# Four attention steps with token pairs on a partition and products in quarters, and one store moved to ScalarE's queue

## The chip, the core and the metric

The kernel runs on one core of a Trainium2 chip. The metric is device microseconds from start to end of one execution; smaller is better. Engines are named as in the profile: PE is TensorE's matmul side and PEld its weight loads, DVE is VectorE, ACT is ScalarE, POOL is GpSimd and SP is SyncE, which only issues transfers. PEq, SPq and so on are the engines' instruction queues.

## What is computed

Retention (linear attention with a decay for each head) runs over 4 batches, 8 heads, 768 tokens and 64 features. Its output, with the heads side by side, is the input `x` of a mixture of experts: 3072 tokens of 512 features, 8 experts, one expert for each token.

```
state = gamma * state + outer(k[t], v[t])        # for each batch and head, 64 x 64
y[t]  = scale * q[t] @ state
x     = y with heads side by side                # (3072, 512)
e     = argmax(x @ w_gate);  gate = softmax(x @ w_gate)[e]
out   = gate * (relu(x @ w1[e]) @ w2[e])
```

All operands are f32. What is timed here lies almost wholly in the attention stage and in the hand-over to the first expert.

## The kernel before

The decay is split in two: q is multiplied by a rising power of gamma (with the scale) and v by a falling one, both from a table `dec`, so that a step only has to do plain products and a causal mask.

**Steps.** `STEPS` is 12. A step `s` takes 128 tokens of two batches: `where[s] = (m, b1, e)`, where `b1` picks the batches 2*b1 and 2*b1+1, and chunk 2*m+e is a run of 128 tokens. q is loaded for both chunks of an `m` at once, 256 tokens with two neighbours to a partition; k and v are loaded by the chunk, one token to a partition. Steps 0 and 1 are chunks 0 and 1 of the batches 0 and 1; steps 9 and 11 are chunk 5, the last one, of the batches 0, 1 and of the batches 2, 3.

What one step does, for each of its two batches `b`:

- `load` brings q, k and v on SP's queue, some steps ahead. A k or v load is 256 KB, 128 partitions by 8 heads by 64 features, so the runs in DRAM are 64 features long, 256 bytes. A q load has runs of 512 bytes.
- `scale_q` and `scale_v` (lines L521, L527) multiply by the decay, on POOL except for the first.
- `turn_q` and `turn_k` (matmuls at L537, copies by ACT at L550 and L556) bring q and k to features-on-partitions.
- `scores` (L569) makes 64x64 products k.q for each head, on quarters of the array; `mask` (L573, DVE) applies the causal mask and writes `am`.
- `with_state` (L592) adds q times the old state to the output `y`, on quarters of the array.
- `next_state` (L605) makes k.v over 128 tokens, on column halves of the array (128x64); DVE adds it to the state (L609, L611). The last chunk needs none.
- `within` (L623) adds v times `am` to `y`, also on column halves with all 128 tokens; ACT copies `y` to `xT` (L626, L629).
- `to_rows` (L634, DVE) and `store` (L641, SP's queue, four DMAs of 128 KB) write x to DRAM as `x_d`.
- Every second step `logits` (L652, L662) makes the router's logits.

The order on each engine is that of the code (a schedule written by hand); all loads and stores of x share SP's queue, in order. DMAs take eight semaphores in turn, and a DMA waits for the one that had its semaphore before.

**The hand-over.** After steps 5, 9 and 12 (`NEXT`) a `place` generator works out, piece by piece, which expert each token goes to and where; DVE does most of it (L680 to L751) and PE the counts `rk` (L705 to L709) and `found` (L747). With the tokens of steps 0 to 8 placed, step 10 ends with `sources` (`src_e`, L188 to L191), and POOL gathers the first 256 tokens of expert 0 from `x_d` (the early gather, L177, into `xs`). The gather waits for all stores of the steps 0 to 8. Behind it on POOL stand a one-element memset (L756), which holds back the second part of expert 0's first weights until the gather is issued, and the scaling of v for step 11. In step 11 ACT copies the gathered rows to `xe` (L863), PE turns them (`tre`, L807) between the two halves of `within`, and the first layer of expert 0 follows (`hp`, L264). Then come the rest of the routing, the second layer (`yp`, L389) and the other experts.

## Time and profile before

| what | value |
|---|---|
| time of three runs | 450.75 us median (449.15, 450.75, 458.32) |
| the profiled execution | 448.83 us, of which the span of the instructions is 446.9 us |
| busy, share of the span | PE 425.1 us (95%), PEld 84%, POOL 61%, DVE 53%, ACT 28% |
| granted TensorE clock, mean | 0.985 |
| DMA | 80.73 MB, mean 181 GB/s; in the first quarter of the span the DMA engines are busy nine tenths or more in nearly every slice |

The table by stages, the chain of work that ended last and the waits say where an engine stood still; the rows that matter are shown with the prediction. In rows of instructions the columns are the start, the time busy, engine, line, operation, output and input, and in brackets the idle time before it and what ended that.

### The profile page before, as it was taken

What the parts mean: (1) busy time and instruction counts of PE and PEld (TensorE: products, weight loads), DVE (VectorE), ACT (ScalarE), POOL (GpSimd) and SP (SyncE); (2) the same over time, 40 slices, a digit from 0 to 9 for tenths busy, and PEclk for the clock granted to TensorE, in tenths of its full rate; (3) what the DMA queues carried; (4) which work ended last, traced back from release to release, by engine and by line L of the source; (5) the groups of instructions that cost most, each with busy time, mean ns of one, the idle gap of its engine ahead of it and who ended that gap; (6) DMA issues with size and microseconds to landing.
All of it is one profiled execution on the core that took longest, in us unless ns stands there. A gap on an engine that the chain in (4) does not pass through costs nothing.

```text
span 446.9 us, 10588 instructions
## 1 busy us (share of the span) xinstructions
PE 425.1 (95%) x4027; PEld 373.8 (84%) x4027; DVE 237.1 (53%) x541; ACT 124.0 (28%) x285; POOL 271.9 (61%) x226
## 2 busy tenths in 40 slices
PE   7899999997999999999999999799999999999992
PEld 5799888885788779689999998697999999699681
DVE  4454686878389938525652662255356435534320
ACT  2356445362421211313210321024122114112310
POOL 4467525553037479386457958894789698579111
PEclk9999999999899999999999999989999999999997
DMA  9999999988972799368125942774297258120001
GB/s 197 235 238 204 238 243 220 230 195 221 281 230 75 258 396 336 91 240 273 29 69 152 376 128 49 237 289 107 71 301 249 55 167 340 32 91 0 5 29 53
DMA packets 113327, 80.73 MB, mean 181 GB/s; under 512 B 56874, under 2 KB 97834, under 8 KB 113200
## 3 DMA queue, kind: packets, MB, share of 16 engines
q1 hardware_dynamic: 104336, 65.31, 52.5%
q0 software_dynamic: 5520, 12.60, 8.6%
q10 hardware_dynamic: 3344, 1.36, 1.3%
q8 instruction: 52, 0.85, 0.8%
q14 instruction: 75, 0.61, 0.5%
HBM read 60.88 MB, written 15.99 MB: 172 GB/s over the span
## 4 chain that ended last, share of the span: by engine, by line
PE 86%; DMA 4%; DVE 3%; ACT 1%; POOL 1%; SPq 1%; issue 1%; another core or an unknown queue 0%; POOLq 0%; DVEq 0%; ACTq 0%
PE p L343 26%; PE p L389 19%; PE p L277 8%; PE p L264 6%; PE p L983 6%; PE y L623 4%; PE sc L569 4%; PE new L605 2%; PE trk L537 2%; PE yp L389 2%; PE trq L537 2%; PE y L592 2%; DMA w2t<-in_moe_w_dram 2%; DMA q<-in_q_dram 1%; PE parts L652 1%
## 5 line engine op out<-in xcount | busy, mean ns | idle before, releaser
L177 POOL DMA_INDIRECT xs<-x_d,src x30 | 31.9, 1064 | 21.2 <-issue 7.5
L347 DVE TENSOR_TENSOR hT<-p,q 128x196 f32<-128x196 f32 (+5 forms) x72 | 25.5, 359 | 31.2 <-PE p L343 30.5
L573 DVE TENSOR_TENSOR am<-sc,causal 128x512 f32<-128x512 f32 x48 | 29.9, 682 | 20.0 <-PE sc L569 20.0
L343 PE MATMUL p<-t,w1t 128*128 128x196 f32 (+5 forms) x192 | 37.0, 337 | 3.3 <-DVE q L347 3.3
L436 POOL DMA_INDIRECT out_dram<-o,dst x20 | 19.9, 995 | 32.3 <-ACT o L285 12.0
L527 POOL TENSOR_TENSOR vs<-v,dec 128x512 f32<-128x512 f32 x21 | 22.9, 1102 | 24.8 <-DMA v<-in_v_dram 15.5
L277 PE MATMUL p<-w2t,hT 128*24 128x128 f32 (+5 forms) x288 | 37.8, 357 | 0.0
L389 PE MATMUL p<-ws,hs 128*128 128x256 f32 x168 | 37.4, 379 | 0.0
L343 PEld LDWEIGHTS p<-t,w1t 128*128 128x128 f32 x192 | 33.3, 195 | 3.5 <-DVE q L347 3.5
L343 PE MATMUL p<-t,s 128*128 128x196 f32 (+5 forms) x192 | 35.8, 329 | 0.0
L389 PEld LDWEIGHTS p<-ws,hs 128*128 128x128 f32 x168 | 31.9, 190 | 4.3
L395 DVE SCALAR_TENSOR_TENSOR q<-p,gate,q 128x256 f32<-128x256 f32 x28 | 12.8, 480 | 40.3 <-PE p L389 21.1
L521 POOL TENSOR_TENSOR qs<-q,dec 128x512 f32<-128x512 f32 x22 | 22.6, 1054 | 19.0 <-DMA q<-in_q_dram 9.2
L305 POOL TENSOR_TENSOR ws<-w2t,ws 128x1024 f32<-128x1024 f32 x14 | 32.9, 2353 | 0.5
L305 POOL TENSOR_TENSOR ws<-w2t 128x1024 f32<-128x1024 f32 x14 | 33.1, 2364 | 0.1
L347 DVE TENSOR_TENSOR q<-p,q 128x196 f32<-128x196 f32 (+5 forms) x48 | 16.8, 358 | 30.5 <-PE p L343 20.4
L343 PEld LDWEIGHTS p<-t,s 128*128 128x128 f32 x192 | 32.4, 190 | 0.0
L277 PEld LDWEIGHTS p<-w2t,hT 128*24 128x24 f32 (+5 forms) x288 | 18.6, 122 | 16.2 <-issue 15.0
L395 DVE SCALAR_TENSOR_TENSOR o<-p,gate,q 128x256 f32<-128x256 f32 x21 | 10.1, 484 | 34.0 <-PE p L389 25.5
L389 PE MATMUL p<-w2t,hT 128*128 128x256 f32 x112 | 26.9, 381 | 0.1
L569 PE MATMUL sc<-qT,kT 64*64 64x128 f32 x768 | 24.4, 273 | 2.3 <-ACT kT L556 2.3
L983 PE MATMUL p<-hT,w2t 128*128 128x136 f32 (+2 forms) x192 | 25.7, 295 | 0.0
(221 smaller groups left out, 884.6 us busy)
## 6 DMA issues: line engine op xcount, KB each, us to landing
w1t<-in_moe_w_dram SPq DMA_DIRECT2D x7, 2048.0 KB
w2t<-in_moe_w_dram SPq DMA_DIRECT2D x7, 2048.0 KB
k<-in_k_dram SPq DMA_DIRECT2D x24, 256.0 KB
v<-in_v_dram SPq DMA_DIRECT2D x24, 256.0 KB
x_d<-xg SPq DMA_DIRECT2D x48, 128.0 KB
q<-in_q_dram SPq DMA_DIRECT2D x11, 512.0 KB
xs<-xs SPq DMA_DIRECT2D x80, 64.0 KB
w2t<-in_moe_w_dram SPq DMA_DIRECT2D x2, 1024.0 KB
```

The source lines that it names most:

```text
L177: nc.gpsimd.indirect_dma_start(out=xs[:, t, :], out_offset=None, in_=x_d[0:rows, :], in_offset=bass.IndirectOffsetOnAxis(ap=idx[:, t : t + ...
L264: nc.tensor.matmul(hp, lhsT=w1t[:, 0, dt, ts(f, P)], rhs=xT[:, dt, n0:n], start=(dt == 0), stop=(dt == DT - 1))
L277: nc.tensor.matmul(y[j * z : j * z + m, 0:c], lhsT=hT[:, f, t * P + r0 : t * P + r0 + m], rhs=w2t[:, 0, f, ts(j, c)], start=(i == 0), stop ...
L305: by.tensor_tensor(out=ws[i], in0=sums[i][0], in1=sums[i][1], op=ALU.subtract)
L343: nc.tensor.matmul(rows(y), lhsT=a(d, f), rhs=b(d), start=start and d == 0, stop=d == 1, skip_group_check=True)
L347: nc.vector.tensor_tensor(out=to, in0=rows(y), in1=rows(plus), op=ALU.add)
L389: nc.tensor.matmul(y, lhsT=a[:, f, :], rhs=b[:, f, :], start=start and f == 0, stop=f == FH - 1, skip_group_check=True)
L395: nc.vector.scalar_tensor_tensor(out=to, in0=y, scalar=g[i], in1=plus, op0=ALU.mult, op1=ALU.add)
L527: by.tensor_tensor(out=vs, in0=got, op=ALU.mult, in1=inner(dec[:, ts(NC + 2 * where[s][0] + where[s][2], H)], D))
L569: nc.tensor.matmul(sc[j][keys, a, :], lhsT=kT[r, a, keys], rhs=qT[r, a, :], start=True, stop=True)
L573: nc.vector.tensor_tensor(out=am[j], in0=sc[j], in1=middle(causal[:, :], HP), op=ALU.mult)
L983: nc.tensor.matmul(y, lhsT=w2t[:, 0, f, ts(dt, P)], rhs=hT[:, f, EARLY : EARLY + m], start=(i == 0), stop=(i == FT - 1))
```

## The change

- **Layout.** In the steps 0, 1, 9 and 11 (`PAIRED`) the k and v of both batches share one tile: 64 partitions for batch 0 and 64 for batch 1, two neighbouring tokens to a partition, so that the runs in DRAM are 512 bytes. What was "batch b" in these steps becomes "token parity i" for the tiles, and the batch becomes a half of the partitions. All other steps keep their layout, with one tile for both batches.
- **Scaling.** In the four steps POOL scales k (into `ks`) and not v, ahead of the turn; v goes into the products as it was loaded. `dec` has 48 more columns for that. `scale_both(11)` leaves its place behind the early gather and stands at the start of step 10.
- **Products in quarters.** `next_state` (steps 0 and 1) and `within` (all four) have 64 tokens of one batch on a half of the partitions, so that each product is 64x64 on a quarter of the array, in twice as many matmuls; `new` takes two PSUM banks. A second mask `causal2` is made by four more selects on POOL at the start. `within` begins with i = 1 there and ACT copies `y` only at its end.
- **Order.** `y` is kept by batch (bank b) in all steps, so `within` of the other steps does batch 0, copies it, then does batch 1. In the four steps `with_state` stands inside the second `scores`. In step 0 both q are turned first, with DVE scaling both, then both k; `turn_k` of step 1 stands ahead of `within` of step 0.
- **Store.** `store(8)`, the last that the early gather needs, is issued from ACT's queue at the end of step 9, and no longer from SP's queue in the middle of it.

```diff
+PAIRED = (0, 1, 9, 11)
...
+            if s in PAIRED:
+                nc.sync.dma_start(raw[nm, s][ts(b, P // 2), :].rearrange("p (h r) -> p h r", h=H),
+                                  got.rearrange("h (t e) d -> t h (e d)", e=2))
...
+        def scale_kv(s, i, by=nc.gpsimd):
+            c = 2 * where[s][0] + where[s][2]
+            got, nm, c = ("k", "ks", 2 * NC + 2 * CP.index(c) + i) if s in PAIRED else ("v", "vs", NC + c)
+            if i == 0:
+                raw[nm, s] = att.tile([P, 2 * H * D], F32, tag="vs", name=nm)
+            by.tensor_tensor(out=half_of(nm, s, i), in0=half_of(got, s, i), op=ALU.mult, in1=inner(dec[:, ts(c, H)], D))
...
+            if s in PAIRED:
+                new = [ps(*tag, "new")[:, 0 : HP * D].rearrange("p (a d) -> p a d", a=HP) for _ in range(2)]
+                for i in range(2):
+                    kt, vs = keys(s, i), values(s, i)
+                    for a in range(HP):
+                        for b, j in ((0, 0), (1, 1), (0, 1), (1, 0)):
+                            h, rows = 2 * a + j, ts(b, P // 2)
+                            nc.tensor.matmul(new[b][ts(j, D), a, :], lhsT=kt[rows, h, :], rhs=vs[rows, h, :],
+                                             start=(i == 0 and a == 0), stop=(i == 1), skip_group_check=True)
...
+                    if s in PAIRED:
+                        for b, j in ((0, 0), (1, 0), (0, 1), (1, 1)):
+                            rows = ts(b, P // 2)
+                            nc.tensor.matmul(place_of(y, b, a, j), lhsT=vs[rows, 2 * a + j, :], rhs=am[i][0][j][rows, a, :],
...
-                scale_both(STEPS - 1)
...
+            if s + 1 in PAIRED:
+                scale_both(s + 1)
...
-                if s == NEXT[NR - 1]:
-                    store(s - 1)
...
+            if s == NEXT[NR - 1]:
+                store(s - 1, nc.scalar)
```

How the rows stand on the engines, at three places. In them `trq` and `trk` are the turns of q and k, `sc` the scores, `new` the next state, `y` the output, `lg` and `parts` the logits, `tre` the turn of the gathered rows, `hp` the first layer.

PE, step 0, from its first turn to its first product for `y`; before:

```order
L537 MATMUL trq<-ident,qs 128x128 x8
L537 MATMUL trk<-ident,k 128x128 x4
L569 MATMUL sc<-qT,kT 64x128 x16
L537 MATMUL trq<-ident,qs 128x128 x8
L537 MATMUL trk<-ident,k 128x128 x4
L569 MATMUL sc<-qT,kT 64x128 x16
L605 MATMUL new<-vs,k 64x64 x16
L623 MATMUL y<-am_196,vs 64x128
```

and now, up to the turns of step 1's k and the first product:

```order
L568 MATMUL trq<-ident,qs 128x128 x16
L568 MATMUL trk<-ident,ks 128x128 x8
L602 MATMUL sc<-qT,kT 64x128 x32
L648 MATMUL new<-v,ks 64x64 x32
L568 MATMUL trk<-ident,ks 128x128 x8
L680 MATMUL y<-am_243,v 64x128 x2
```

Both batches' q stand ahead of any k, `new` has 32 matmuls where it had 16, and the turns of step 1's k have come ahead of `y`.

PE, step 11, from the scores to the turn of the gathered rows (the matmuls of `y` that only repeat are left out); before:

```order
L569 MATMUL sc<-qT,kT 64x128 x32
L763 LDWEIGHTS ones_b
L763 MATMUL tot<-acc,ones_b 128x2
L652 MATMUL parts<-xT,wg 32x256 x8
L592 MATMUL y<-qT,state_1981 64x128 x16
L662 MATMUL lg<-ident,lgT 128x128 x4
L623 MATMUL y<-am_2036,v 64x128
```

and now:

```order
L602 MATMUL sc<-qT,kT 64x128 x28
L624 MATMUL y<-qT,state_2023 64x128 x16
L602 MATMUL sc<-qT,kT 64x128 x4
L823 LDWEIGHTS ones_b
L823 MATMUL tot<-acc,ones_b 128x2
L713 MATMUL parts<-xT,wg 32x256 x8
L723 MATMUL lg<-ident,lgT 128x128 x4
L680 MATMUL y<-am_2115,v 64x128 x2
```

The product with the state has moved from between `parts` and `lg` into the scores, and `y` takes v as it was loaded.

POOL, from the last piece of the routing in step 9 to the early gather; before:

```order
L696 CAST told<-less 128x8
L527 TENSOR_TENSOR vs<-v,dec 128x512 x2
L177 DMA xs_112<-x_d,src_e 128x512 x2
L756 MEMSET w1t 1x1
L527 TENSOR_TENSOR v<-v,dec 128x512 x2
```

and now:

```order
L757 CAST told<-less 128x8
L554 TENSOR_TENSOR ks<-k,dec 128x512 x2
L554 TENSOR_TENSOR vs<-v,dec 128x512 x2
L192 DMA xs_74<-x_d,src_e 128x512 x2
L817 MEMSET w1t 1x1
```

Step 11 is scaled ahead of step 10, and nothing is left behind the gather. On ACT the four stores now stand between the copies of step 9's `y` and the turns of step 11's k.

More of the change, by code (lines that the diff above doesn't have):

```diff
@@ L37, in decay_table @@
     back = [gamma ** -(P * c + i + 1) for c in range(NC)]
+    two = 2 * (i % (P // 2))
+    back += [gamma ** -(P * c + two + e + 1) for c in CP for e in range(2)]
     return np.concatenate(on + back, 1).astype(np.float32)
@@ L96 @@
     x_d = dram.tile([N, Q * DT * L], F32, tag="x_d", name="x_d")
-    dec = const.tile([P, 2 * NC * H], F32, tag="dec", name="dec")
+    dec = const.tile([P, 2 * (NC + len(CP)) * H], F32, tag="dec", name="dec")
     wg = const.tile([P, DT, P // DT], F32, tag="wg", name="wg")
     ident = const.tile([P, P], F32, tag="ident", name="ident")
-    ones = const.tile([P, P], F32, tag="ones", name="ones")
+    causal2 = const.tile([P, 2, P], F32, tag="causal2", name="causal2")
+    first = ctx.enter_context(tc.tile_pool(name="first", bufs=1))
+    xs2 = [first.tile([P, TC, Q * DT * L], F32, tag=f"xs{i}", name=f"xs{i}") for i in range(2)]
+    ones = xs2[0][:, 0, 0:P]
     causal = const.tile([P, P], F32, tag="causal", name="causal")
@@ L114 @@
                             pattern=[[1, P]], channel_multiplier=-1)
+    for b in range(2):
+        for e in range(2):
+            rows = ts(b, P // 2)
+            nc.gpsimd.affine_select(out=causal2[rows, e, :], in_=ones[rows, :], compare_op=ALU.is_ge, fill=0.0, base=-e,
+                                    pattern=[[1, P]], channel_multiplier=-2)
     nc.gpsimd.memset(ones_b, 1.0)
@@ L170, in weights @@
         return weights1(pool, e), weights2(pool, e)
-    first = ctx.enter_context(tc.tile_pool(name="first", bufs=1))
-    xs2 = [first.tile([P, TC, Q * DT * L], F32, tag=f"xs{i}", name=f"xs{i}") for i in range(2)]
     def gather(xs, idx, tiles, rows=N):
@@ L496 @@
             warm(P)
-        where = [(s // 4, s // 2 % 2, s % 2) for s in range(STEPS)]
+        where = [place_of_step(s) for s in range(STEPS)]
         raw, front, state, x = {}, {}, {}, {}
@@ L605, in next_state @@
                         nc.tensor.matmul(new[ts(j, D), b, a, :], lhsT=kt[:, h, :], rhs=vs[:, h, :], start=True, stop=True)
-            old = state.get(b1)
-            state[b1] = att.tile([P, 2, HP, D], F32, tag=f"state{b1}", name=f"state{b1}")
-            if old is None:
-                nc.vector.tensor_copy(state[b1], new)
-            else:
-                nc.vector.tensor_tensor(out=state[b1], in0=new, in1=old, op=ALU.add)
+            add(now, new, old)
         def within(s, y, am, between=lambda: None):
@@ L635, in to_rows, with store @@
                                     x[s][:, :, b, :].rearrange("p a (r l) -> p a r l", l=L))
-        def store(s):
+        def store(s, queue=nc.sync):
             m, b1, e = where[s]
@@ L825 @@
                     scale_q(s + 2, b)
-            if s + 2 < STEPS and s != NEXT[NR - 1]:
+            if s + 1 < STEPS and s + 1 not in PAIRED and s != NEXT[NR - 1]:
                 scale_both(s + 1)
@@ L831, with old_state @@
                 nc.gpsimd.memset(xs2[s % 2], 0.0)
+            y = outputs()
+            def old_state():
+                if where[s][0] or where[s][2]:
+                    with_state(s, y)
             if s:
-                am = [scores(s, b) for b in range(2)]
+                am = [scores(s, 0), scores(s, 1, old_state if s in PAIRED else lambda: None)]
                 am[0][1]()
@@ L843 @@
                 logit = logits(steps)
-            if where[s][0] or where[s][2]:
-                with_state(s, y)
+            if s not in PAIRED:
+                old_state()
             def ahead():
@@ L890 @@
             step(s, "b")
+            if s == 0:
+                ahead()
             within(s, y, am, early_rows if s + 1 == STEPS else lambda: step(s, "w"))
@@ L952 @@
         pair(hTa, wa[1], S, T, oa, egates, lambda: fetch_ahead(which, 0),
-             lambda name: att.tile([P, FH * P], F32, tag="v", name=name, bufs=8)[:, 0:DH], some,
+             dict(zip(("m10", "m11", "u20", "u21", "u3"), (pe[:, ts(i, DH)] for pe in [
+                 att.tile([P, 2 * FH * P], F32, tag="v", name="pe", bufs=4) for _ in range(3)] for i in range(2)))).get, some,
              (("sc", 4), ("sc", 4), ("y", 2), ("y", 2), ("tr", 2), ("tr", 2)))
```

144 lines of the change are left out of this document (83 added, 61 removed).

## The prediction

> **What bounds the kernel now.** I read the table by stages first, then the chain that ended last, then the rows at the places where that chain leaves PE. The stages are cut where PE begins step 1's scores (18.17), where DVE takes up the routing of steps 5 to 8 (91.08), where PE begins step 11 (104.32), at the first `hp` (117.01) and at the third product of `yp` (136.51).
>
> ```profile
> 0.00:18.17 18.17, 14.09 (x166) 10.56 (x166) 6.90 (x16) 6.62 (x11) 7.60 (x24) 1.00 1.08 220
> 18.17:91.08 72.91, 72.07 (x1593) 64.23 (x1594) 47.01 (x93) 35.53 (x65) 40.60 (x43) 1.00 1.01 227
> 91.08:104.32 13.24, 11.61 (x233) 10.21 (x231) 12.14 (x38) 6.00 (x12) 5.54 (x9) 1.00 0.88 200
> 104.32:117.01 12.69, 9.72 (x160) 7.25 (x158) 7.61 (x25) 4.06 (x7) 4.34 (x5) 0.87 0.88 246
> 117.01:136.51 19.50, 19.30 (x105) 15.74 (x104) 14.05 (x45) 5.58 (x14) 6.34 (x9) 1.00 0.78 224
> 136.51:446.90 310.39, 298.28 (x1776) 265.79 (x1776) 149.34 (x326) 66.16 (x178) 207.46 (x139) 0.98 0.49 161
> ```
>
> A row gives the stretch, its length, the busy time of PE, PEld, DVE, ACT and POOL, the granted clock, the DMA share and GB/s. Steps 1 to 8 are PE's own time: 72.07 of 72.91 us are busy. The DMA engines are full there too (1.01), so a transfer that gets shorter gives nothing at once; it lands earlier. Behind 117.01 the change edits little (two temporaries share a tile), and PE is busy 19.30 of 19.50 us, so what is won or lost ahead of `hp` should reach the end unchanged. Room is at the head (4.1 us without PE), in step 10 (1.6 us) and in step 11 (3.0 us, at a clock of 0.87). For step 11 the chain says why:
>
> ```profile
> 104.45 3.58 DMA v<-in_v_dram
> 108.03 1.24 POOL xs L177
> ...
> 110.67 2.02 POOL v L527 x2
> 112.73 1.02 PE y L623 x8
> 113.75 1.91 PE tre L807 x8
> 115.66 1.35 PE y L623 x16
> 117.01 1.92 PE hp L264 x8
> ```
>
> The early gather starts at 108.03, v of step 11 is scaled behind it, and PE's products wait for that. The rows of the timeline around it show what the gather itself stood waiting for:
>
> ```profile
> 94.53 1.31 DVE L634 STREAM_TRANSPOSE xg<-xT 128x512 f32<-128x512 f32 x2
> 95.43 8.35 SPq L641 DMA_DIRECT2D x_d<-xg  x12
> 104.36 0.17 DVE L191 TENSOR_SCALAR src_e<-tok_e 128x2 uint32<-128x2 f32 x1
> 112.60 0.62 ACT L863 COPY xe<-xs 128x512 f32<-128x512 f32 x1 [4.37 <-DMA xs<-x_d,src_e]
> 113.87 0.62 ACT L863 COPY xe<-xs 128x512 f32<-128x512 f32 x1 [0.65 <-DMA xs<-x_d,src_e]
> ```
>
> The rows to gather were known at 104.53. Step 8's x was ready at 95.84, but its store is the last four of the twelve that SP worked off until 103.78, in line behind older ones; so the 3.5 us to 108.03 are the landing of these stores (the chain puts them down to a v load issued next, which shares semaphores with them).
>
> **The change, part by part.**
>
> *Transfers.* The first row below is a stretch with 256-byte packets alone, the second one (14.4 to 16.4 us) with 512-byte packets nearly alone.
>
> ```profile
> DMA packets 3720, 0.82 MB, mean 205 GB/s; under 512 B 3720, under 2 KB 3720, under 8 KB 3720
> DMA packets 1144, 0.59 MB, mean 297 GB/s; under 512 B 16, under 2 KB 1143, under 8 KB 1143
> ```
>
> k and v of a paired step are 1 MB: 5.1 us at 205 GB/s, 3.5 us at 297. Two such steps stand at the head of the queue (3.2 us) and two near its end (3.2 us). Everything that SP issues behind step 1 comes about 3 us earlier, and the v of step 10, for which POOL and then PE waited, 4 to 5 us.
>
> *Head.* These rows of the chain and of the timeline carry the old and the new one:
>
> ```profile
> 2.40 5.78 DMA q<-in_q_dram
> 4.37 1.59 DVE L521 TENSOR_TENSOR qs<-q,dec 128x256 f32<-128x256 f32 x4 [2.90 <-DMA q<-in_q_dram]
> 7.06 0.64 ACT L550 COPY qT<-trq 128x512 f32<-128x512 f32 x1 [4.47 <-PE trq L537]
> 7.80 0.59 ACT L556 COPY kT<-trk 128x512 f32<-128x512 f32 x1
> 12.16 1.04 POOL L527 TENSOR_TENSOR vs<-v,dec 128x512 f32<-128x512 f32 x1 [1.79 <-DMA v<-in_v_dram]
> 12.26 1.10 PE sc L569 x32
> 13.36 1.08 PE new L605 x32
> ```
>
> Before, the second q landed at 8.18, as the 1280th KB. Now both halves of k stand ahead of it: 1536 KB at the higher rate, some 0.7 us later, about 8.9. DVE then scales its last half (0.8 us), PE turns it, ACT copies (0.64): 10.5. POOL's four more selects end at 4.5, k has landed by 7.2, `ks` is done at 9.3, off the path. The turns of k and the copy to `kT` (0.59) bring the first scores to 11.4 and their end to 13.3, where they ended at 13.36 before. `new` (priced below at 1.91) ends at 15.2. k of step 1 lands near 13 and is scaled by 15.1, so that its turns run 15.2 to 16.2, `y` until 18.1, and step 1 starts then: **0.0 us** against 18.17. Bounds: 0.7 earlier if `new` costs what it did; 2 us later if k of step 1 lands 2 us later than I have it, since POOL's scaling and the turns are in its line.
>
> *Products in quarters.* Step 3 has all kinds of product in a row:
>
> ```profile
> 33.40 1.91 PE sc L569 x64
> 35.31 0.87 PE y L592 x32
> 36.18 1.00 PE parts L652 x16
> 38.20 0.44 PE lg L662 x4
> 40.39 1.08 PE new L605 x32
> 41.47 1.75 PE y L623 x32
> ```
>
> The trace counts two passes to a matmul. A quarter pass costs 29.8 ns in the scores and 27.2 ns in `y L592`. `y L623` has 32 passes on column halves, 54.7 ns each; in quarters 64 passes at 29.8 ns are 1.91 us, 0.16 more. `new` has 32 passes of half the length at 33.8 ns each; in quarters 64. No row shows quarter passes of 64 columns. If four of them run side by side as the long ones do, the cost stays 1.08 us; if a pass takes no less time than any quarter pass of the trace does, it is 1.91. I take 1.91, since 1.08 would need 16.9 ns a pass, half of the shortest seen in these rows. The Trainium skill ("TensorE: Matmul & The Clock Gate", Back-to-back issue gap) gives a floor of about 25 ns from start to start however short a matmul is: by it `new` would be estimated at 1.6 us and the sum 0.3 us lower; no row here decides between them. Step 1 is on PE's dense stretch: +0.83 and +0.16, **+1.0 us**. Step 9's +0.16 falls into PE's idle time of step 10, where DVE is last.
>
> *DVE's chain.* From 91.08 to 104.53 DVE sets the pace (12.14 of 13.24 us busy, ending with `src_e`). It starts 1.0 later. One piece of it was slow before, while POOL scaled v of step 9 beside it; the second row is the same operation later, alone:
>
> ```profile
> 91.66 0.72 DVE L681 TENSOR_TENSOR dl<-lg,mx 128x64 f32<-128x64 f32 x1
> 121.32 0.21 DVE L681 TENSOR_TENSOR dl<-lg,mx 128x48 f32<-128x48 f32 x1
> ```
>
> POOL scales k of step 9 already in step 8 now: **-0.5 us** (bounds 0 and 0.5). `src_e` ends at 105.0.
>
> *Store and gather.* ACT issues store(8) behind the copies of step 9's `y`, about 97 to 99.5, and it lands some 2 to 3 us later, ahead of 105.0. Behind it on ACT wait the copies of step 11's `kT`, needed by PE at 104.8: hidden, with 4 us to spare. SP's last half of store(7), v of step 11 and the first weights wait for semaphores that these four DMAs hold, until about 102; the weights are needed at `hp`, so that is hidden as well. The gather starts at 105.1 and not at 108.03: **-2.9 us** with the two terms above in it.
>
> *From the gather to `hp`.* Before, 8.98 us. The two halves of the gathered rows landed 4.57 and 5.84 us behind its start, so now `xe` is there at 110.3 and 111.6. PE starts step 11 at 104.8; scores with the state 2.8, `parts` 1.2 with the small count, the copy of the logits, now bare, 0.6, `lg` 0.44, half of `y` 0.95: 110.9, so nothing waits for v any more. The turns take 0.5 each at full clock, the second from 111.6; the other half of `y` ends at 113.1, where `hp` starts: 8.0 us, **-1.0 us**. It rests on the clock, too:
>
> ```profile
> 113.00:114.00 1.00, 1.00 (x10) 0.67 (x7) 0.00 (x0) 0.35 (x2) 0.00 (x0) 0.50 1.10 368
> ```
>
> After PE's pause the clock was half and the turns took 1.91 us; with PE at work until 110.9 I take it as full. If it is not, 1 us is lost.
>
> **Sum.** `hp` at 113.1 against 117.01: -3.9 us, so 448.83 - 3.9 = 444.9 for the profiled execution (span 443.0). That execution is the lowest of those shown; the other two near it, 449.15 and 450.75, are on average 1.1 above it. I predict 446.
>
> **Rivals.**
>
> 1. *Quarter passes of 64 columns run side by side.* `new` stays at 1.08, step 1 starts 0.7 earlier and costs 0.16 more. DVE's chain is 1.0 earlier than before instead of 0.5 later, so 443.4 in the sum, 444.5 as a time. For it: quarters do overlap in two rows. Against: 16.9 ns a pass is seen nowhere. 17%.
> 2. *The store gains nothing by its new queue.* store(8) moves at the pace of what SP has queued, or ACT is held by a semaphore whose last DMA is still in SP's line; then the gather starts near 108.0 as before and `hp` 8.0 later, at 116.0: 447.8, or 449 as a time. For it: the DMA share is 0.88 in that stretch and ACT's four DMAs wait for DMAs of SP's. Against: 3 us less of line by then. The Trainium skill ("DMA: Bandwidth & Descriptors", Issuing engines are not separate DMA queues) says that all queues share the same 16 engines and a second issuer saves only issue time, which is this rival; the row of twelve stores shows that time to be 8.35 us. 18%.
> 3. *Slower: quarters with all tokens of two batches do not overlap.* Passes cost 54.7 ns in `y` and 33.8 in `new`. Step 0 gives +1.75, step 1 +2.83, step 9 +1.3 in DVE's chain, step 11 +0.8: `hp` at 118.8, 1.8 late, 450.6, or 451.7 as a time. It loses from some 47 ns a pass on, on a line between 29.8 (-3.9) and 54.7 (+1.8). Against: two kinds of quarter product run below 30 ns. 10%.
>
> My forecast has 55%.
>
> **Range.** The forecast with its bounds (head -0.7 to +2, clock +1) is 445 to 449; to hold eight in ten it reaches over rivals 1 and 2 and their spread: 442 to 450.5. 2% is 9 us (about what a measurement of this kernel can tell from no change), and no case comes near it: within 92%, faster 5%, slower 3%.
>
> **What would show it.** Step 1's scores start near 18.1; its `new` takes 1.9 us and `y` 1.9; `src_e` ends near 105, the gather starts with it and no longer waits for a DMA; no half clock around step 11; `hp` near 113. I am wrong if PE waits for `trk` of step 1 or 9, if the gather still waits for stores, or if the stages behind `hp` change in length.

## The result

The changed kernel takes 452.25 us (median of 20 runs), the kernel before 449.87 us (20 runs on the same chip): a ratio of 1.0132 with a 95% interval of 1.0098 to 1.0165. I had said 446, 442 to 450.5; the change made the kernel slower by some 1%, where I expected 1% faster. In some executions the granted clock is lower and the time some per cent longer; the ratios leave these out, and the profiles of b_store and best6 below are such executions, so that their ratios count and their stages are only a hint.

The profiled execution after took 452.17 us (span 450.5), the one before 448.83 (446.9). These two differ by 3.6 us of span, the medians by 2.4; the ratio stands for some 5.9 us. What follows explains the 3.6; the two profiles don't say where the rest of the 5.9 lies. The table by stages, cut at the same events as before:

```profile
0.00:21.66 21.66, 15.91 (x231) 12.01 (x235) 9.78 (x21) 4.76 (x7) 12.05 (x31) 0.84 1.03 245
21.66:95.61 73.95, 71.75 (x1666) 64.18 (x1659) 50.35 (x95) 36.87 (x67) 36.98 (x39) 1.00 0.95 231
95.61:110.11 14.50, 12.22 (x265) 10.50 (x263) 13.02 (x37) 6.00 (x12) 5.23 (x9) 1.00 0.60 147
110.11:120.14 10.03, 8.61 (x192) 6.40 (x190) 7.45 (x22) 3.37 (x6) 2.33 (x3) 1.00 0.68 222
120.14:139.90 19.76, 19.76 (x108) 16.36 (x108) 14.78 (x50) 6.15 (x15) 6.56 (x10) 1.00 0.76 205
139.90:450.50 310.60, 297.67 (x1775) 263.57 (x1773) 148.69 (x326) 65.84 (x178) 207.01 (x138) 0.99 0.48 161
```

| stage | before | after | difference |
|---|---|---|---|
| head, until PE begins step 1 | 18.17 | 21.66 | +3.49 |
| steps 1 to 9, until the routing chain on DVE | 72.91 | 73.95 | +1.04 |
| routing chain, until step 11 | 13.24 | 14.50 | +1.26 |
| step 11, until `hp` | 12.69 | 10.03 | -2.66 |
| `hp` to the third `yp` | 19.50 | 19.76 | +0.26 |
| rest | 310.39 | 310.60 | +0.21 |

In the table above, the row "steps 1 to 9" hides two opposite terms: step 1 takes 1.34 us and step 8 1.29 us longer, while steps 4 and 6 take 6.63 and 6.64 us instead of 7.06 and 8.12.

**The head.** The chain that ended last (first fence), the timeline (second) and three stretches of the table by windows (third; the third number from the end is the granted clock):

```profile
8.54 2.16 DVE qs L546 x2
...
10.75 1.54 PE trq L568 x6
12.29 1.71 PE trk L568 x8
13.99 1.83 PE sc L602 x32
```

```profile
8.19 2.22 POOL L554 TENSOR_TENSOR ks<-k,dec 128x512 f32<-128x512 f32 x2 [3.63 <-DMA k<-in_k_dram]
8.54 2.82 DVE L546 TENSOR_TENSOR qs<-q,dec 128x256 f32<-128x256 f32 x4 [1.17 <-DMA q<-in_q_dram]
9.56 0.69 PE L568 MATMUL trq<-ident,qs 128*128 128x128 f32 x2 [3.12 <-DVE qs L546]
```

```profile
8.00:9.00 1.00, 0.00 (x0) 0.00 (x0) 0.46 (x1) 0.00 (x0) 0.81 (x1) 0.84 1.20 286
9.00:14.50 5.50, 4.44 (x28) 3.67 (x32) 3.05 (x5) 1.68 (x3) 1.75 (x3) 0.50 1.23 245
15.00:16.00 1.00, 1.00 (x36) 1.00 (x32) 0.15 (x1) 0.00 (x0) 1.00 (x2) 0.75 1.15 341
```

The second q landed at 8.5, forecast was about 8.9. But DVE needs 2.82 us for its four products, 1.59 before: POOL scales k over the first two. PE has nothing to do for 3.12 us, and its clock is half from 8.7 to 15.5 us, so that eight turns of k take 1.71 us and half the scores 1.83, where 1.0 to 1.1 each is usual.

**Step 1.** From the chain:

```profile
28.59 1.09 PE new L648 x64
29.68 1.31 PE y L680 x48
30.99 0.92 issue
31.91 0.67 PE y L680 x16
```

`new` in quarters takes no longer than in halves (1.09 us, 17 ns a pass). Inside `y` PE stands still for 0.92 us and waits for nothing that the trace shows (such a row is called "issue"); before, no such gap stood in step 1. Some 0.4 us more goes ahead of the products with the state: a weight load waits 0.39 us for ACT's copies of step 0's `y`, all three of which now come at its end.

**Steps 8 to 10.** The timeline:

```profile
80.85 5.08 DVE L792 TENSOR_SCALAR here<-rrow,prow 128x128 bf16<-128x128 bf16 x10
81.79 2.09 POOL L554 TENSOR_TENSOR ks<-k,dec 128x512 f32<-128x512 f32 x2 [4.14 <-issue]
83.84 4.04 POOL L546 TENSOR_TENSOR qs<-q,dec 128x512 f32<-128x512 f32 x4
86.58 0.85 PE L808 MATMUL found<-val,here 128*128 128x160 bf16 x10 [1.13 <-DVE am L608]
...
98.42 0.22 DVE L751 TENSOR_REDUCE gate<-ex 128x8 f32<-128x64 f32 x1 [1.00 <-ACT ex L743]
100.41 2.05 POOL L554 TENSOR_TENSOR ks<-k,dec 128x512 f32<-128x512 f32 x2
100.93 0.54 DVE L778 TENSOR_TENSOR acc<-acc,seen 128x8 bf16<-128x8 bf16 x1
101.47 1.02 DVE L783 TENSOR_SCALAR prow<-ranks 128x8 int32<-128x8 int32 x1
102.41 2.25 POOL L554 TENSOR_TENSOR vs<-v,dec 128x512 f32<-128x512 f32 x2
102.61 1.15 DVE L785 TENSOR_TENSOR at<-ohs,is_col 128x256 f32<-128x256 bf16 x1
```

Before, the same ten `here` and the same `gate` stood like this; `acc`, `prow` and `at` took 0.17, 0.17 and 0.43:

```profile
77.66 3.35 DVE L731 TENSOR_SCALAR here<-rrow,prow 128x128 bf16<-128x128 bf16 x10
93.89 0.22 DVE L690 TENSOR_REDUCE gate<-ex 128x8 f32<-128x64 f32 x1 [0.51 <-ACT ex L682]
```

Each long row of the kernel after stands beside a scaling on POOL. The first rows cost PE 1.13 us in step 8, the others lie in the chain to `src_e`.

**Step 11.** The gather follows the rows to gather at once (timeline); behind it PE's chain has three short gaps (chain):

```profile
110.31 0.17 DVE L206 TENSOR_SCALAR src_e<-tok_e 128x2 uint32<-128x2 f32 x1
110.78 1.24 POOL L192 DMA_INDIRECT xs<-x_d,src_e  x1 [6.12 <-DMA w1t<-in_moe_w_dram]
```

```profile
111.87 0.23 issue
...
112.69 0.19 issue
...
113.35 0.30 issue
```

### The profile page after: what moved, and what is told of

Its sections match the earlier page's. It is cut to its first block, busy times and chain, and to the rows that moved or that the text cites. A ratio compares the mean times of both kernels' runs of the same rounds, so it can differ in the third digit from the quotient of the medians.

```text
span 450.5 us, 10959 instructions
## 1 busy us (share of the span) xinstructions
PE 425.9 (95%) x4219; PEld 373.0 (83%) x4219; DVE 244.1 (54%) x547; ACT 123.0 (27%) x284; POOL 270.2 (60%) x229
## 3 DMA queue, kind: packets, MB, share of 16 engines
q10 hardware_dynamic: 4432, 1.91, 1.7%
## 4 chain that ended last, share of the span: by engine, by line
PE 88%; DVE 5%; DMA 2%; issue 2%; ACT 1%; SPq 1%; POOLq 0%; DVEq 0%
PE p L358 25%; PE p L404 19%; PE p L292 8%; PE p L279 6%; PE p L1049 6%; PE sc L602 4%; PE hp L279 3%; PE yp L404 3%; PE y L684 3%; PE trk L568 2%; PE trq L568 2%; PE y L624 2%; PE new L659 1%; PE y L680 1%; PE parts L713 1%
## 5 line engine op out<-in xcount | busy, mean ns | idle before, releaser
L410 DVE SCALAR_TENSOR_TENSOR q<-p,gate,q 128x256 f32<-128x256 f32 x28 | 12.8, 480 | 42.5 <-PE p L404 29.5
L410 DVE SCALAR_TENSOR_TENSOR o<-p,gate,q 128x256 f32<-128x256 f32 x21 | 10.2, 484 | 33.8 <-PE p L404 28.5
L669 ACT COPY xT<-y 64x512 f32<-64x512 f32 (+1 forms) x36 | 20.9, 581 | 24.3 <-PE y L684 17.9
L554 POOL TENSOR_TENSOR vs<-v,dec 128x512 f32<-128x512 f32 x16 | 16.6, 1055 | 17.1 <-DMA v<-in_v_dram 17.0
L1049 PEld LDWEIGHTS p<-hT,w2t 128*128 128x128 f32 x192 | 25.5, 190 | 0.0
```

The lines of the kernel that those rows point to most:

```text
L410: nc.vector.scalar_tensor_tensor(out=to, in0=y, scalar=g[i], in1=plus, op0=ALU.mult, op1=ALU.add)
L669: nc.scalar.copy(out=x[s][rows, :, b, :], in_=y[b][other, :, :])
L1049: nc.tensor.matmul(y, lhsT=w2t[:, 0, f, ts(dt, P)], rhs=hT[:, f, EARLY : EARLY + m], start=(i == 0), stop=(i == FT - 1))
```

## The experiments

Four questions: the head, PE's gap in step 1, POOL beside DVE in steps 8 to 11, and the store. The chips differ between groups, so ratios go against runs of the kernel before on the same chip, and stages are read from each run's profile. One profile stands for each run, and small differences between two of them are no effect of an edit: best2 and best2_sp differ in nothing ahead of step 9, yet the routing chain begins 2.03 us apart (90.92 and 92.95), and a gap of 1.77 us in step 4 of best2_sp makes most of it. Ratios of different chips can't be compared finely either: after, h_dvek and s_sp bring `hp` within 1 us of each other and have 1.0132, 1.0065 and 1.0076.

| run | step 1 begins | step 1 takes | chain begins (`lg`) | `lg` to end of `src_e` | `src_e` to `hp` | `hp` | ratio (95%) |
|---|---|---|---|---|---|---|---|
| before | 18.17 | 9.40 | 91.08 | 13.45 | 12.41 | 116.94 | 1 |
| after | 21.66 | 10.74 | 95.61 | 14.87 | 9.59 | 120.07 | 1.0132 (1.0098-1.0165) |
| h_warm | 19.67 | 11.35 | 94.22 | 14.86 | 9.23 | 118.31 | 1.0131 (1.0048-1.0214) |
| h_dvek | 20.99 | 11.58 | 96.03 | 14.85 | 9.59 | 120.47 | 1.0065 (1.0031-1.0099) |
| h_both | 19.20 | 12.17 | 97.62 | 14.88 | 9.59 | 122.09 | 1.0094 (1.0055-1.0133) |
| p_oldhead | 18.55 | 9.17 | 93.20 | 14.87 | 9.59 | 117.66 | 1.0035 (1.0001-1.0069) |
| p_01 | 22.58 | 12.40 | 98.57 | 14.21 | 9.68 | 122.46 | 1.0085 (1.0042-1.0127) |
| e_fill | 21.40 | 9.24 | 94.01 | 14.88 | 8.82 | 117.71 | 1.0083 (1.0041-1.0125) |
| r_noks | 20.36 | 10.74 | 92.63 | 14.12 | 8.56 | 115.31 | 0.9973 (0.9930-1.0015) |
| r_early | 20.94 | 11.57 | 96.25 | 12.96 | 9.62 | 118.83 | 1.0037 (0.9998-1.0076) |
| best1 | 18.05 | 9.30 | 93.94 | 13.93 | 9.60 | 117.47 | 1.0025 (0.9981-1.0069) |
| best2 | 18.42 | 9.17 | 90.92 | 16.30 | 9.80 | 117.02 | 1.0023 (0.9969-1.0077) |
| best2_sp | 18.54 | 9.56 | 92.95 | 17.39 | 9.77 | 120.11 | 0.9995 (0.9954-1.0037) |
| best6 | 23.79 | 10.20 | 95.61 | 14.13 | 8.15 | 117.89 | 1.0078 (1.0042-1.0113) |
| best4 | 18.00 | 9.20 | 92.32 | 14.49 | 9.58 | 116.39 | 1.0039 (1.0003-1.0076) |
| best5 | 18.09 | 9.39 | 94.34 | 14.14 | 8.16 | 116.64 | 0.9979 (0.9933-1.0025) |
| s_sp | 20.36 | 11.30 | 95.07 | 14.86 | 9.60 | 119.53 | 1.0076 (1.0029-1.0122) |
| b_store | 18.66 | 9.98 | 92.62 | 15.15 | 8.81 | 116.58 | 1.0013 (0.9965-1.0061) |

### The head: h_warm, h_dvek, h_both, p_oldhead

h_warm, in the changed kernel:

```diff
             scale_q(0, b, nc.vector, 2)
+            for _ in range(3 * b):
+                warm(512)
             turn_q(0, b, 2, (nc.scalar.copy, nc.vector.tensor_copy))
```

> Three more idle products on PE between the two turns of q, so that PE doesn't pause while DVE scales the second q. Theory A (after PE's pause the granted clock is half from 9 to 14.7 us, and that stretches the turns of k from 1.02 to 1.91 us, the last turns of q and the scores): the clock stays 1.0, step 0's scores end near 14.5 instead of 16.6, and step 1's scores start near 20.0 instead of 21.55; DVE's scaling of the second q stays at 2.82 us. Rival B (the longer order alone costs the 3.4 us: both q and both k must be scaled and turned before any score): the clock is full but step 1 starts within 0.5 us of 21.55.

h_dvek:

```diff
-        scale_both(0)
...
         scale_q(0, 1, nc.vector, 2)
+        for i in range(2):
+            scale_kv(0, i, nc.vector)
         turn_q(0, 1, 2, (nc.scalar.copy, nc.vector.tensor_copy))
```

> Step 0's k is scaled by DVE behind its second q, so that POOL does nothing while DVE scales. Theory (POOL's scaling of k from 8.19 to 10.41 holds up DVE's four products of the second q, 2.82 us for them instead of 1.57): they take 1.6 us again, the turns of q end about 1.2 us earlier, and step 1's scores start near 20.5, though k is now scaled by 11.7 instead of 10.4. Rival (DVE is slow there for another cause, such as a q that lands in pieces): the four still take 2.8 us, k is ready at 12.9, and step 1 starts at 23 or later.

h_both has both edits.

> Both mends of the head in one kernel: three idle products on PE while it waits for the second q, and step 0's k scaled by DVE behind that q instead of by POOL beside it. If the clock and the lock-out are the two costs of the head and they add: the clock stays at 1.0, DVE needs 1.6 us for the second q, and step 1 starts near 18.7 to 19.3 (old head: 18.1 to 18.6; the three idle products alone: 19.67). Rival (the longer order costs the rest, and k by DVE comes later than k by POOL): step 1 starts at 19.7 or later, no earlier than with the idle products alone.

p_oldhead: `PAIRED = (9, 11)`, with the loads, order and scalings of the head as before the change.

> Only steps 9 and 11 have two tokens to a partition; steps 0 and 1 stand as in the kernel before, with its loads and its order at the head; the store of step 8 stays on ACT's queue. If the head and step 1 are where the time went (3.38 and 1.5 us by the two traces): step 1's scores start near 18.2 as before, the routing chain starts near 91.5, hp near 116, and the time is 4 to 5 us under the changed kernel's, 1 under the kernel's before or level with it. Rival (the longer stages of steps 8 to 10 follow from the later transfers of steps 0 and 1 or from their PE time, and the gain in step 11 rests on the shorter transfers of steps 0 and 1): step 1 starts at 18.2, but hp at 117.5 or later.

The same stretch of windows in h_warm, and DVE's first two products for the second q in h_both:

```profile
9.00:14.50 5.50, 5.04 (x81) 3.58 (x81) 3.41 (x7) 1.72 (x3) 1.85 (x2) 1.00 1.23 266
```

```profile
8.44 0.76 DVE L546 TENSOR_TENSOR qs<-q,dec 128x256 f32<-128x256 f32 x2 [1.05 <-DMA q<-in_q_dram]
```

With PE kept at work the clock stays at 1.00 and step 1 begins at 19.67; the six runs with this head and no mend of the clock began it between 20.36 and 22.58 (p_01's 22.58 has a gap of 1.14 us in it; best6's head is another one). So the half clock costs 0.7 to 2 us, by when it falls and how long it lasts: 6.83 us from 8.67 on in the changed kernel, 3.41 us from 10.60 and 10.71 on in s_sp and r_noks, whose heads are the same program and begin step 1 at 20.36. The 2 us are the dear end of it. With nothing on POOL beside them two products take 0.76 us, where the changed kernel's first two took 2.16. In h_dvek itself this bought little: the second half of q landed only at 10.5, PE paused as long, and the clock was half from 11.26 to 14.68; h_both, with both mends, begins at 19.20, 0.5 ahead of h_warm. The old head stands at 18.0 to 18.7 in seven runs. So of 3.5 us the clock is the largest part, POOL's holding up of DVE about half a microsecond once the clock is mended, and 0.5 to 1.2 us the longer order (both q before any score).

p_oldhead, where step 1 begins at 18.55 and takes 9.17 us, is rid of three quarters of the loss up to `hp` (0.72 us of 3.13 are left; its ratio is 1.0035). Still `hp` comes at 117.66 and not at 116, as its rival had said: its chain takes 14.87 us as in the changed kernel. The two mends of the longer head don't show in the time: h_both's `hp` is the second latest of the table. Its lead is lost in steps 1 and 8. In step 8, which takes 11.12 us there and 8.62 in the changed kernel, `here` takes 6.04 us beside POOL, PE waits 2.08 us, and the clock is half from 87.21 to 90.62. What went wrong behind the head is the next question.

### PE's gap in step 1: p_01, e_fill, and the other runs

p_01: `PAIRED = (0, 1)`; steps 9 to 11 and the store as in the kernel before.

> Only steps 0 and 1 have two tokens to a partition; steps 9 to 11, their scalings and the store on SP's queue stand as in the kernel before. If the head, step 1 and POOL's scaling of k of step 9 are the losses: step 1 starts at 20.4 to 21.7, step 8 takes 7.3 us again, the chain of routing 13.3, and the transfers of the first steps, some 3 us ahead, let v of step 11 land early; hp near 118.5 to 119.5, the time 1.5 to 2.5 us over the kernel's before. Rival (the lead of the transfers is the gain, and steps 9 and 11 only cost): hp at 117 or earlier and the time level with or under the kernel's before.

e_fill, in p_oldhead, at the start of steps 0 and 1:

```diff
+            if s < 2:
+                quarters(32)   # 32 products 64x64x16 on idle data, one bank for each row half
             y = outputs()
```

> Steps 9 and 11 paired, steps 0 and 1 as in the kernel before, and ahead of each of these two 32 idle products of 64 x 64 x 16 on PE, which write nothing that is used: as many instructions as the quarters of steps 0 and 1 add. Theory (PE runs out of fetched instructions): a gap of 0.9 to 2.5 us with nothing to wait for appears in step 1, some 16 passes ahead of the end of its y, which is in halves here, and ends about 1 us behind the landing of the packet of the instruction queue; step 1 takes 10.5 to 12 us from scores to scores instead of 9.2. Rival (the gap belongs to the quarters): no gap, step 1 takes 9.2 to 9.5 us beside the idle products, which stand ahead of its scores and cost 1 to 2 us there.

In all runs with steps 0 and 1 paired (here h_warm, h_both, p_01, s_sp) the gap is there, and always at the same place of PE's program:

```profile
28.21 1.49 PE L680 MATMUL y<-am,v 64*64 64x128 f32 x48
31.17 0.67 PE L680 MATMUL y<-am,v 64*64 64x128 f32 x16 [1.47 <-issue]
```

```profile
30.42 1.49 PE L680 MATMUL y<-am,v 64*64 64x128 f32 x48
34.49 0.67 PE L680 MATMUL y<-am,v 64*64 64x128 f32 x16 [2.57 <-issue]
```

```profile
27.61 1.47 PE L680 MATMUL y<-am,v 64*64 64x128 f32 x42
30.51 0.77 PE L680 MATMUL y<-am,v 64*64 64x128 f32 x19 [1.43 <-issue]
```

The first is s_sp, the second p_01: 48 passes of `y`, then the gap, then 16. The third is h_warm, which has three more products (six passes) ahead of it: the gap comes after 42 passes, and the last three of 64 have a row of their own. After h_both's three it is 42 too. A wait on data would not move by six passes. The queues of the DMA engines show what does come in steps of the program, here in the changed kernel from 29.5 to 31.0:

```profile
q8 instruction: 1, 0.02, 3.9%
```

One packet of 16 KB, busy for 0.9 us (3.9% of 16 engines in 1.5 us), on a queue that the profile calls "instruction". Narrower windows put its start at 29.7. Found in the same way in ten profiles (before, where the gap is the 0.72 us in step 6; after; h_warm, h_dvek, h_both, p_01, r_noks, r_early, s_sp, best6), such a packet landed 1.3 to 1.55 us ahead of the end of the gap, while the gaps' ends lie between 30.5 and 34.5 us in the paired ones. It holds for more than step 1: between 10 and 125 us of the 18 profiles PE has 24 gaps of over 0.32 us that wait for nothing, in 15 of the profiles, and each ends 1.28 to 1.59 us behind the landing of a 16-KB packet of this queue. Some shorter ones, as the three in step 11, have no such packet just ahead. I take it that PE has run out of fetched instructions there; the packets and the place of the gap speak for it, though it is inferred and no run took a packet away.

The expectation for e_fill failed in part: step 1 took 9.24 us without a gap. In step 0 it has one:

```profile
15.20 1.91 PE L691 MATMUL y<-am,vs 128*64 128x128 f32 x31
17.86 0.32 PE L691 MATMUL y<-am,vs 128*64 128x128 f32 x1 [0.74 <-issue]
28.79 1.92 PE L691 MATMUL y<-am,vs 128*64 128x128 f32 x32
```

It stands near the end of step 0's `y`, where the changed kernel (0.33 us, 9 passes ahead of the end) and p_01 (1.14) have their first one. So the number of instructions alone brings the first gap, and not the second; why the second packet comes late in the paired steps stays open. What it costs is in the table: step 1 takes 9.2 to 10.0 us unpaired and 10.2 to 12.4 paired. A quicker head may only wait longer (h_both 2.25 us, ending at 30.86; the changed kernel 0.92, ending at 31.91), though r_noks, 1.3 us ahead, waits 0.92 as well.

p_01 says the same of the whole: the two paired steps at the head alone bring `hp` to 122.46. That is 3 us later than expected, with four gaps of this kind (1.14, 2.57, 0.45 and 0.79 us) and a half clock from 111.45 to 114.86. Its rival, that the lead of the transfers is a gain, fell for the whole; a part of it may be real, since in the nine kernels with steps 0 and 1 paired step 6 takes 6.6 us, and 6.6 to 8.4 in the others.

### POOL beside DVE: r_noks, r_early, best1, best2, best6, best4, best5

r_noks, in the changed kernel, leaves out the factor on k in steps 9 and 11 (`keys` gives the raw k there, its tokens in another order), so that its output is not that of the program:

```diff
-            if s + 1 in PAIRED:
+            if s + 1 in PAIRED and s < 8:
                 scale_both(s + 1)
```

> Leaves out the scaling of k in steps 9 and 11 on POOL (the products take the raw k, and its tokens in another order): PE and DVE have the same work, POOL 4 us less. Theory (POOL's scaling holds up DVE's operations beside it): the ten rows of here in step 8 take 3.3 us instead of 5.08 and PE no longer waits 1.1 us for am behind them; of the routing chain acc 0.54, prow 1.02 and at 1.15 go back to 0.17, 0.17 and 0.43, unless the scaling of v of step 10 moves beside them; the chain starts near 94.3 and the rows to gather are known 2 to 3 us earlier than 110.48. Rival (DVE is slower there for its own order, or PE is what it waits for): here stays at 5 us and the chain ends within 0.5 us of 110.48.

r_early:

```diff
-                raw[nm, s] = att.tile([P, 2 * H * D], F32, tag="vs", name=nm)
+                raw[nm, s] = raw["v", s] if s in (8, 10) else att.tile([P, 2 * H * D], F32, tag="vs", name=nm)
...
+            if s == NEXT[NR - 1]:
+                scale_both(STEPS - 1)
+                scale_both(s + 1)
```

> The changed kernel with POOL's scalings of late moved clear of DVE's small operations: v of steps 8 and 10 is scaled in place, so that k of step 9 needs no buffer that is still read and is scaled near 78 to 80, ahead of here, and k of step 11 and v of step 10 in step 9, ahead of the routing chain or beside its first operations, not beside acc, prow and at. The head is unchanged. Lock-out theory: here x10 takes 1.9 to 3.4 us instead of 5.08, acc, prow and at 0.17, 0.17 and 0.43, val starts 1.5 us earlier behind own, and from step 1's start to hp it takes 3.5 to 5 us less than the changed kernel's 98.4. Rival (PE and ACT hold the chain, DVE's slow rows only fill its slack): the rows get short and hp moves by less than 1.5 us.

The rows of r_noks, then those of r_early:

```profile
79.22 1.90 DVE L794 TENSOR_SCALAR here<-rrow,prow 128x128 bf16<-128x128 bf16 x10
97.40 2.05 POOL L554 TENSOR_TENSOR vs<-v,dec 128x512 f32<-128x512 f32 x2
98.46 1.01 DVE L785 TENSOR_SCALAR prow<-ranks 128x8 int32<-128x8 int32 x1
```

```profile
101.56 0.17 DVE L778 TENSOR_TENSOR acc<-acc,seen 128x8 bf16<-128x8 bf16 x1
101.72 0.17 DVE L783 TENSOR_SCALAR prow<-ranks 128x8 int32<-128x8 int32 x1
```

Without k's scaling beside them the ten `here` take 1.90 us instead of 5.08, and `at`, now alone, 0.42; `prow`, beside v's scaling, still takes 1.01. Step 8 takes 7.33 us again, as before, and not 8.62. The time falls: against h_dvek on the same chip, which differs in the head, the ratio is lower by 0.0092, some 4 us, and `hp` comes 5.2 us earlier; how much of the time comes from the other output, with other routing behind it, wasn't separated. The rows of `here` themselves need no such care. Over all 18 profiles the ten take 1.70 to 1.90 us where POOL scales nothing or next to nothing beside them, 2.74 to 3.35 beside two scalings, 4.23 to 5.20 beside three or four, and 6.04 in h_both. In r_early no scaling stands beside `acc`, `prow` and `at`, all are short (`at` 0.42), and the chain takes 12.96 us, 1.9 less than in the changed kernel and 0.5 less than before. In step 8 r_early gained nothing: k of step 9 is scaled from 78.2, but the q of step 10 then follows on POOL beside `here`, which takes 5.20. By its own measure the expectation failed: from step 1 to `hp` it takes 97.89 us, 0.5 less than the changed kernel's 98.41 and not 3.5 to 5, and `hp` moved by 1.24 us, which the rival allowed. But steps 1 and 8 are 0.83 and 0.48 us longer there; from `lg` to `hp`, the part where the rows got short, it takes 22.58 us for 24.46. There they did not only fill slack.

The Trainium skill ("SBUF — State Buffer", SBUF: two separate sides) says that VectorE and GpSimd share one port pair as an exclusive lock, held for a whole instruction, against VectorE operations with two SBUF inputs or in a two-port mode. The rows agree with it: `am`, one of whose two inputs lies in PSUM, takes 1.28 us for two beside POOL (at 103.68 in the changed kernel) and alone (at 106.28).

best1 is r_early with the head of p_oldhead.

> The moved scalings together with the head of the kernel before: two tokens to a partition in steps 9 and 11 only, store on ACT. If head and lock-out are the two losses and they add: step 1 starts at 18.2 to 18.6, the routing chain at 90 to 91, hp near 112 to 113, the time 4 to 5 us under the kernel's before (ratio 0.990). Rival (the longer transfers of steps 0 and 1 bring k and v too late for the earlier places, so POOL blocks on them and told comes late): the chain gains under 1 us over the run with the old head alone, ratio 0.998 to 1.002.

Here `here` takes 1.70 us, but k of step 9, in line on POOL behind v of step 8, which landed late, was only scaled by 82.7: a weight load of PE waits 2.55 us for it, the clock is half from 81.85 to 85.27, and the chain begins at 93.94. Its rival was right. best2 has only step 11 paired (`PAIRED = (11,)`, old head):

> Only step 11 has two tokens to a partition, store of step 8 on ACT; head, steps 0, 1 and 9 as in the kernel before. If what is good in the change is step 11's unscaled v and the store, and what is bad the head, step 1 and the scaling of k of step 9: step 1 starts near 18.3, the routing chain near 91, POOL's scaling of k of step 11 may hold DVE up by some 0.7 us there, hp at 114.5 to 116, the time 1 to 2.5 us under the kernel's before (ratio 0.995 to 0.998). Rival (without the transfers' lead, k of step 11 and v of step 10 land too late for POOL, so told and val wait): src_e behind 106.5 and hp at 117 or later, ratio 1.000 or over.

```profile
98.48 3.19 POOL L554 TENSOR_TENSOR ks<-k,dec 128x512 f32<-128x512 f32 x2 [2.69 <-DMA k<-in_k_dram]
100.73 2.12 PE L568 MATMUL trk<-ident,ks 128*128 128x128 f32 x8 [3.05 <-POOL ks L554]
100.90 3.65 DVE L792 TENSOR_SCALAR here<-rrow,prow 128x128 bf16<-128x128 bf16 x8
```

The chain begins at 90.92, and then loses 2.85 us against before: PE waits 3.05 us for k of step 11, and `here` takes 3.65 us instead of 1.38. Its rival was right. That is the new link: before, k went from its landing straight to PE, and POOL scaled v, which is needed later.

To part this link from the pairing, best6, best4 and best5 turn k as it lies, a head's two tokens to a block, and scale v in place where the kernel before does:

```diff
+                for a in range(HP):
+                    nc.tensor.transpose(tr[:, a, :], got[:, 2 * a + i, :], ident)
+                for n in range(2):
+                    nc.scalar.copy(out=front[s, n][ts(i, D), :, :], in_=tr[ts(n, D), :, :])
```

> All four steps paired as in the changed kernel, the same bytes and quarters, but k is turned as it lies (a block is one head with its two tokens; ACT copies each half to its place, four copies of 64 rows instead of two of 128) and v is scaled in place by POOL where the kernel before scales it. Theory (POOL's scaling of k, ahead of the turn and beside DVE, costs steps 8 to 10): step 8 takes 7.3 us instead of 8.6, lg to src_e 13.3 to 13.8 instead of 14.7; the head gains up to 1 us, as nothing stands beside DVE's second q, step 1 keeps its gap; hp at 116.5 to 118 instead of 120.07, the time 2 to 3.5 us under the changed kernel's. Rival (quarters and the head cost it all, POOL's work is only moved from k to v): hp within 1 us of 120.07.

> The same with only steps 9 and 11 paired and the head of the kernel before. If the theory of POOL's scaling of k holds, the shorter transfers of steps 9 and 11 are left as a gain: step 1 at 18.3, routing chain from 90.5 to 91.5, src_e at 104 to 105, the gather 0.5 to 2 us behind it, hp at 113.5 to 115.5: 1.5 to 3.5 us under the kernel before, ratio 0.993 to 0.997. Rival (ACT's four copies for two hold up kT and ex, and v of step 11, scaled behind the gather again, holds PE up): hp at 117 or later, ratio 1.000 or over.

> The same with steps 3, 5, 7, 9 and 11 paired. If transfers bind the kernel before in steps 1 to 8 (DMA share 1.01) and PE has few gaps, three more pairs bring k and v 1.5 us earlier each at a cost of 0.2 us of PE each: the routing chain starts at 90 to 91.5 and the stores land earlier; hp at 112.5 to 115. Rival (every paired step brings PE to a gap for want of instructions, or ACT's copies hold up kT): steps 3 to 7 take 1 to 2 us longer each, the chain starts at 93 or later and the time is over the kernel's before.

best6's step 8 takes 7.33 us and its ten `here` 1.90; its `hp` is at 117.89 in spite of a head of 23.79 us. With the old head, best4's chain takes 14.49 us, since the scaling of v of step 10 still stands beside `prow` and `at` (1.02 and 1.15 us); two gaps (1.14 and 0.82 us in steps 4 and 6) delay its beginning. best5, with three (1.19, 1.20 and 0.80 us in steps 4, 6 and 8), begins the chain only at 94.34, as its rival said, though its time is not over the kernel's before. Both `hp` miss what was expected (113.5 to 115.5 and 112.5 to 115). best4's `hp` is 0.55 us ahead of the kernel's before and best5's 0.3; the times are 1.0039 and 0.9979, and none of the 16 kernels beats the kernel before by what can be measured.

### The store: s_sp, b_store, best2_sp

```diff
+                if s == NEXT[NR - 1]:
+                    store(s - 1)
...
-            if s == NEXT[NR - 1]:
-                store(s - 1, nc.scalar)
```

> The changed kernel with the last store ahead of the early gather issued by SP again, where the kernel before has it. If the new queue is what frees the gather (forecast -2.9 us): the gather waits for stores again and starts 1.5 to 3 us behind the rows to gather, hp comes 1.5 to 3 us later behind them than the 9.8 us of the changed kernel, and v of step 11 and the first weights are no longer held back. Rival (SP is some 4 us earlier anyway by the shorter transfers, so the store lands in time on either queue): the gather starts within 0.5 us of the rows to gather and hp stays at 9.8.

> The kernel before with nothing changed but that store on ACT's queue, behind step 9's copies. If the queue alone gives the gain: the gather starts right behind the rows to gather (3.5 us earlier than before), but v of step 11 still lands and is scaled behind it on POOL, so hp comes 2 to 3 us earlier: ratio 0.994. Rival (the gain needs the shorter transfers as well: the store's DMAs queue behind SP's, or SP, held by shared semaphores, brings v and the weights later): the gather gains under 1 us, or hp's line shifts to v and the time does not fall.

> The same with the store of step 8 on SP's queue, where the kernel before has it. If the queue matters where the rows to gather are known early (near 105): the gather waits for stores until some 107.5 to 108 and hp comes 1 to 2 us later than with the store on ACT. Rival (the stores land when the transfers let them, on either queue): the gather starts within 0.7 us of the run with the store on ACT.

s_sp, with the store back on SP:

```profile
109.76 0.17 DVE L206 TENSOR_SCALAR src_e<-tok_e 128x2 uint32<-128x2 f32 x1
110.23 1.24 POOL L192 DMA_INDIRECT xs<-x_d,src_e  x1 [6.11 <-DVE src_e L206]
```

The gather follows the end of `src_e` by the same 0.30 us on either queue, and `hp` by 9.60 (after: 9.59). best2_sp shows it once more (0.29), and p_01, with the store on SP and v of step 11 scaled, too (9.68). b_store, the queue alone, is level (1.0013); in its profile the gather starts 1.38 us behind `src_e`, while SP issues its own eight stores until 105.08. So the queue is not what freed the gather. In the kernel before, the stores had landed by 108.03; here the rows are known only at 110.48. The 2.66 us "won" in step 11 are slack that the earlier losses used up. At most some 0.9 us of it is seen elsewhere: best4 and r_noks start the gather at 107.1. What the queue would do where the rows are known by 105 wasn't seen: in no other run were they known ahead of 106.7.

## Why the prediction was wrong

The sum was -3.9 us to `hp`; it came out as +3.1. By its steps:

- **Head, 0.0: failed, measured +3.49.** I wrote that `ks` "is done at 9.3, off the path" (k landed 1 us later than I had it, and `ks` ran from 8.19 to 10.41) and let DVE scale the last half of q in 0.8 us. Both times stood in the working above; that the two would run beside each other, I didn't count, though I had seen a DVE row of 0.72 us beside POOL (`dl`) two paragraphs later. And I asked for PE's clock only in step 11, not in the head, where the new order leaves PE idle for 3.1 us. The bounds (-0.7 to +2) didn't hold it either.
- **`new` in quarters, 1.91: failed, measured 1.09.** Rival 1's mechanism was right: 17 ns a pass. That the shortest pass seen bounds the next was no argument, and the 1.6 us that I gave beside it are too many as well. `y` in quarters was right: 1.31 and 0.67 against 1.91.
- **Step 1, +1.0: size near (+1.34), cause wrong.** None of it is pass time of `new`; 0.92 is the gap, most likely for want of instructions, which is 0.4 to 2.6 us in the other paired runs, and some 0.4 the wait for ACT's copies. Before has one such row (0.72 us in step 6), which I did not ask about.
- **Step 8: not in the sum, measured +1.29.** Steps 4 and 6, also not in it, gave 1.91 us back, of which 0.72 is a gap that the profile before has in step 6. Moving the scaling of k to step 8 was booked only as a relief of step 9's chain. What it stands beside there, `here`, was not looked up.
- **DVE's chain, -0.5: failed, +1.4 from `lg` to `src_e`.** `dl` did shrink from 0.72 to 0.23, and nothing came of it: `gate` waits for `ex`, which stands on ACT behind four copies of q (wait 0.51 before, 1.00 after), so `lg` to `gate` is 2.81 us in both. k of step 11 beside the small operations is the loss.
- **Store and gather, -2.9: the start behind `src_e` was right (0.30 us), the reason wrong.** s_sp shows it: there the rows to gather came 5.4 us later than before, and the gather waited on SP's queue no longer than on ACT's. Rival 2 had the queue right: it gains nothing.
- **Gather to `hp`, -1.0: failed, measured +0.38** (110.78 to 120.14, 9.36 for 8.98). The half clock is gone, as forecast, though not for good: h_dvek, with the same step 11, has it from 110.25 to 113.66. Nothing waits for v; but PE loses 0.72 us in three short gaps that the chain calls issue, inside step 11's scores, and 0.71 waiting for `lgT`, and gets to the turns of the rows only at 118.09.
- **Behind `hp`: right,** +0.26 and +0.21 us.

The range failed for one reason above all: I priced each moved operation by itself, with a bound on its own duration, and none of them by what another engine does beside it. Rival 3, the only one that made the kernel slower (451.7), came near the measured 452.25 by luck: its mechanism did not occur, as quarter passes ran at 17 ns in `new` and 31 in `y`.

## What to carry to other kernels

When work moves on POOL, list what DVE does in that stretch at its new place, row by row; the price of the move is paid there (here 1.29 us in step 8, for two scalings of 1.04 us each). Scale the operand that is needed last: a factor on k stands between its landing and the first product, the same factor on v doesn't. A stage that waits for a fixed event (here stores landed at 108) shows a "gain" as soon as the stages ahead of it get slower; check against a run with the cause removed before booking it.

## What the runs showed of the hardware

- Quarter products of 64 columns run at 17 ns a pass (64 in 1.09 us): four start 6 to 7 ns apart, the next four 38 to 39 ns behind the last of them.
- PE has gaps of 0.3 to 2.6 us in which it waits for nothing that the trace shows, in step 1 at a fixed place of its program. All 24 of over 0.32 us end 1.28 to 1.59 us behind the landing of a 16-KB packet on the queue "instruction". That PE has run dry of instructions is inferred from this.
- A scaling of 1.04 us on POOL stretches DVE operations of 0.17 us to 0.5 to 1.0 each when they meet: ten `here` take 1.70 to 1.90 us alone, 3.35 beside two scalings, 5.08 beside four. `am`, which reads PSUM, is not held up (1.28 us for two, both ways).
- Pauses of PE bring a granted clock of 0.50 for 3.41 us, or for twice that (6.83 us in the changed kernel and p_01, where PE was busy only 2.0 and 2.4 us of the first 3.41). When it begins differs between profiles of the same head (8.67 in the changed kernel, 10.60 in s_sp). The Trainium skill ("TensorE: Matmul & The Clock Gate", What's actually happening) states an idle window of about 3.4 us ahead of the half clock. The length of the half clock agrees with such a window; that the window is idle doesn't, since PE was busy 0.5 to 2.2 us in the 3.41 us ahead of every drop in the first 125 us.
